# Four separate PSUM tiles for the block products of a fused attention and two-layer feed-forward kernel

## The chip, the cores and the metric

The kernel runs on one core of one Trainium2 chip. The metric is the device time of one execution in microseconds (us); less is better. The engines are TensorE (PE, matmuls; PEld is its weight loads), VectorE (DVE), ScalarE (ACT), GpSimd (POOL) and SyncE (SP, which only issues DMA transfers here).

## What is computed

Three steps in a row, all in float32 at the interface:

```
attn:  scores = q @ k^T / sqrt(D) + min(-(cum_i - cum_j), 0), causal, softmax, @ v
       B=2, H=8, S=576, D=64;  cum = cumsum(max(s, 0))
moe:   x = attn as (1152 tokens, 512);  xn = x / rms(x) * rms_g
       h = (silu(xn @ w_gate) * (xn @ w_val)) @ w_out          d_ff = 1536
moe2:  g = u * tanh(softplus(u)), u = h @ w_in;  out = g @ w_out   d_ff = 2048
```

The function `u * tanh(softplus(u))` is called Mish. The change lies in the third step.

## The kernel before

Matrices are held as pairs of numbers, a high and a low part (`xh` and `xl` for the activations, `w[:, 0]` and `w[:, 1]` for a weight unit), so that a product of two matrices takes three matmul passes: high by high, high by low, low by high (`PASS`, L567). The 1152 tokens are three blocks b = 0, 1, 2 of TB = 384 tokens.

The kernel first does the attention for eight pairs of heads, then the first feed-forward step, with the transfers and the unpacking of its weights beside it. All that is finished, and all weights are on the chip, before the part which the change touches.

In the third step the hidden dimension of 2048 is cut into NG = 8 sets (g = 0 to 7) of two chunks of 128. For each set and block three things are done:

- the inner product u (128 hidden rows x 384 tokens, two of them): `h2_mm` (L631), 24 matmuls of 384 columns, into a tile of two PSUM banks, and `mish` (L664) on ACT behind it;
- `mish_split` (L671): ACT casts the result to its high part, DVE subtracts to get the low part. Both go into one of two halves of the buffer `glb`; which half is chosen at L674;
- the out product, `out_mm` (L677): 18 matmuls of 512 columns, which accumulate over all eight sets into three row groups of 128 tokens (`o_t[b]`), each one bank. After set 7, `out_evac` (L694) copies the row groups to SBUF (ACT and DVE in turn) and SP issues the transfers to the output.

Block 0 does its inner products plainly for all eight sets. Blocks 1 and 2 do so only at set 0. For the sets 1 to 7 they are done together by `strassen` (L781), a scheme with seven products in place of eight for the 2 x 2 problem (two hidden chunks by two blocks, both cut in two along the contraction). `product` (L773) is six matmuls of 384 columns. The seven products go into four accumulators a, b, c and d; a, c and d take a second product on top of the first, with reads of the first in between:

1. product a (a11); ACT copies a into p (L792)
2. product b (s2); DVE adds p = p + b
3. product c (s3); DVE adds q = p + c
4. product d (s1); DVE adds q = q + d
5. a takes a12; ACT makes Mish of a (L806)
6. c takes a22, with t4 as its moving operand; DVE adds p + c, ACT makes Mish of it (L810)
7. d takes s4; DVE adds p = p + d, ACT makes Mish of p and q (L814)

The adds all stand on L717, in the helper `add`. The operands s1 to s4 of a set are sums of weight blocks (`s_restore`, `s_sums` on DVE, then `s_hi` on ACT, L767, and `s_lo` on DVE). They are made one set ahead: for the sets 2 to 6, `s_hi(g+1)` and `s_lo(g+1)` are issued in `gaps[0]`, that is behind product 1 of set g, and so ahead of the adds in DVE's queue. t1 to t4 are sums of activation blocks (`t_sums`, `t_split`); t4 lies in the first half of `glb`, and t3 takes the place of a part of block 2's activations, after the last plain product that reads them. In `gaps[3]` stands `mish_split(1, g-1)`. After each set's products comes `out_mm(1, g-1)`.

PSUM has eight banks. In this step they are three tiles of one bank in the pool `psT` (tag T), one of one bank in `psX` (tag X) and two of two banks each in `psS[1]` (tag S), which `banksS` (L558) hands out in turn. Before the change, a and b share one tile of S and c and d the other; the out product of block 0, and then that of block 1, has the three T tiles; that of block 2 has a pair of S and the X tile.

Each engine works off its instructions in the order in which the program issues them. Around the change this order is written out by hand (L988 to L1003 and the loop from L1014). A program adds the semaphores, which guard each tile against reading and overwriting too early.

Of the kernel before, what the change touches and what calls it, by code (L numbers as in the profile page):

```python
# [7 lines left out]
F32 = mybir.dt.float32  # L8
# [24 lines left out]
TB = 384  # L33
# [9 lines left out]
def tile_kernel(ctx: ExitStack, tc: tile.TileContext, kq, qq, v, s, w1, w2, rms_g, out):  # L43
    nc = tc.nc
    sb = ctx.enter_context(tc.tile_pool(name="sb", bufs=1))
    psT = ctx.enter_context(tc.tile_pool(name="psT", bufs=3, space=bass.MemoryType.PSUM))
    psX = ctx.enter_context(tc.tile_pool(name="psX", bufs=1, space=bass.MemoryType.PSUM))
# [6 lines left out]
    def sbt(shape, dt, tag, name):  # L54
        return sb.tile(shape, dt, tag=tag, name=name)
# [502 lines left out]
    def banksS():  # L558
        return psS[1].tile([128, 2, 512], F32, tag="S", name="gv")
# [66 lines left out]
    h2_t, u_t, g2_t, o_t = {}, {}, {}, {}  # L626

    def unit2(n):
        return unit(NU1 + n)

    def h2_mm(b, g):  # L631
        t = banksS()
        h2_t[b, g] = t
        for x in range(2):
            w = unit2(2 * (2 * g + x))
            n = 0
            for c in range(KD):
                for a, r in PASS:
                    nc.tensor.matmul(t[:, x, 0:TB], w[:, a, 128 * c:128 * c + 128],  # L639
                                     xhl[r][:, c, TB * b:TB * b + TB], start=(n == 0), stop=(n == 11))  # L640
                    n += 1

    NG = NF2 // 2
    glb = []
# [6 lines left out]
    def u_at(b, g):  # L651

        if (b, g) in u_t:
            return u_t[b, g]
        if b == 2 and g > 3:
            if not ub:
                ub.append(sbt([128, 4, 2, TB], F32, "w5", "ub"))
            u_t[b, g] = ub[0][:, g - 4]
        else:
            tag = ("mm", "ring8", "ring3", "ring5")[g] if b == 2 else ("hA", "hB")[g % 2] if b else                 ("hA", "hB", "mm")[g % 3]  # L660
            u_t[b, g] = sbt([128, 2, TB], F32, tag, "u")
        return u_t[b, g]

    def mish(b, g):  # L664
        nc.scalar.activation(out=u_at(b, g), in_=h2_t.pop((b, g))[:, :, 0:TB], func=ACTF.Mish)

    def split_pair(h, l, src):
        nc.scalar.copy(out=h, in_=src)  # L668
        nc.vector.tensor_tensor(out=l, in0=src, in1=h.bitcast(F32), op=ALU.subtract)  # L669

    def mish_split(b, g):  # L671
        if not glb:
            glb.append(sbt([128, 2, 2, 2, TB], F32R, "w6", "glb"))
        g2_t[b, g] = gl = glb[0][:, 1 if b == 1 else g % 2]  # L674
        split_pair(gl[:, 0], gl[:, 1], u_t.pop((b, g)))

    def out_mm(b, g):  # L677
        if g == 0:
            if b < 2:
                o_t[b] = [psT.tile([128, 512], F32, tag="T", name=f"o{n}") for n in range(3)]  # L680
            else:
                a0 = banksS()
                o_t[b] = [a0[:, 0], a0[:, 1], psX.tile([128, 512], F32, tag="X", name="o2")]
        gl = g2_t.pop((b, g))
        for tt in range(TB // 128):
            for x in range(2):
                w = unit2(2 * (2 * g + x) + 1)
                for y, (a, r) in enumerate(PASS):
                    nc.tensor.matmul(o_t[b][tt], gl[:, r, x, 128 * tt:128 * tt + 128], w[:, a],  # L689
                                     start=(g == 0 and x == 0 and y == 0), stop=(g == NG - 1 and x == 1 and y == 2))  # L690
# [3 lines left out]
    def out_evac(b):  # L694
        for tt in range(TB // 128):
            if b == 0 and tt < 2:
                if not ob:
                    ob.append(sbt([128, 2, 512], F32, "ring1", "osb"))
                t = ob[0][:, tt]
            else:  # L700
                t = sbt([128, 512], F32, f"r{(2 * b + tt + 2 * (b == 0)) % 4}", "osb")
            rows = slice(b * TB + 128 * tt, b * TB + 128 * tt + 128)

            cols = (slice(0, 256), slice(256, 512)) if (b, tt) == (NB - 1, 2) else (slice(0, 512),)
            for n, cs in enumerate(cols):
                if (tt + n) % 2 == 0:
                    nc.scalar.copy(out=t[:, cs], in_=o_t[b][tt][:, cs])
                else:
                    nc.vector.tensor_copy(out=t[:, cs], in_=o_t[b][tt][:, cs])
                nc.sync.dma_start(out=out[rows, cs], in_=t[:, cs])  # L710


    def quarter(r, c, b):
        return xhl[r][:, 2 * c:2 * c + 2, TB * b:TB * b + TB]

    def add(o, x, y, op=ALU.add):
        nc.vector.tensor_tensor(out=o, in0=x, in1=y, op=op)  # L717
# [28 lines left out]
    def t_split(n):  # L746
        tsum[n] = ((quarter(0, 0, 0), quarter(1, 0, 0)), (quarter(0, 1, 0), quarter(1, 1, 0)),
                   (quarter(0, 0, 2), quarter(1, 0, 2)), (glb[0][:, 0, 0], glb[0][:, 0, 1]))[n - 1]
        split_pair(*tsum[n], tq[n])

    def s_restore(g):

        c_t[g] = sbt([128, 1024], F32, "r1", "c")
        for x in range(2):
            w = unit2(4 * g + 2 * x).bitcast(F32)
            add(c_t[g][:, 512 * x:512 * x + 512], w[:, 0], w[:, 1])

    def s_sums(g):

        a11, a12, a21, a22 = (c_t[g][:, 256 * n:256 * n + 256] for n in range(4))  # L760
        for o, x, y, op in ((a22, a21, a22, ALU.add), (a21, a11, a21, ALU.subtract),
                            (a11, a22, a11, ALU.subtract), (a12, a12, a11, ALU.subtract)):
            add(o, x, y, op)

    def s_hi(g):
        s_t[g] = [sbt([128, 1024], F32R, t, f"s_{t}") for t in (("r0", "ring1"), ("r2", "r3"))[g % 2]]
        nc.scalar.copy(out=s_t[g][0], in_=c_t[g])  # L767

    def s_lo(g):
        h, l = s_t[g]  # L770
        add(l, c_t.pop(g), h.bitcast(F32), ALU.subtract)

    def product(t, A, B, start):  # L773
        n = 0
        for c in range(2):
            for a, r in PASS:
                nc.tensor.matmul(t, A[a][:, 128 * c:128 * c + 128], B[r][:, c], start=(start and n == 0),  # L777
                                 stop=(n == 5), skip_group_check=True)
                n += 1

    def strassen(g, gaps):  # L781

        w1_, w2_ = unit2(4 * g), unit2(4 * g + 2)
        s2, s4, s3, s1 = ([t[:, 256 * n:256 * n + 256] for t in s_t[g]] for n in range(4))
        a11, a12, a22 = ([w[:, a, o:o + 256] for a in range(2)] for w, o in ((w1_, 0), (w1_, 256), (w2_, 256)))
        x = {(c, b): (quarter(0, c, b), quarter(1, c, b)) for c, b in ((0, 1), (1, 1), (1, 2))}
        u1, u2 = u_at(1, g), u_at(2, g)
        p, q = u2[:, 0], u2[:, 1]
        t = banksS()
        a, b = t[:, 0, 0:TB], t[:, 1, 0:TB]  # L790
        product(a, a11, x[0, 1], True)
        nc.scalar.copy(out=p, in_=a)  # L792
        gaps[0]()
        product(b, s2, tsum[2], True)
        add(p, p, b)
        gaps[1]()
        t = banksS()
        c, d = t[:, 0, 0:TB], t[:, 1, 0:TB]
        product(c, s3, tsum[3], True)
        add(q, p, c)  # L800
        gaps[2]()
        product(d, s1, tsum[1], True)
        add(q, q, d)
        gaps[3]()
        product(a, a12, x[1, 1], False)
        nc.scalar.activation(out=u1[:, 0], in_=a, func=ACTF.Mish)  # L806
        gaps[4]()
        product(c, a22, tsum[4], False)
        add(u1[:, 1], p, c)
        nc.scalar.activation(out=u1[:, 1], in_=u1[:, 1], func=ACTF.Mish)  # L810
        gaps[5]()
        product(d, s4, x[1, 2], False)
        add(p, p, d)
        nc.scalar.activation(out=u2, in_=u2, func=ACTF.Mish)  # L814
# [73 lines left out]
    for p in range(NP):  # L888
# [9 lines left out]
        if NP - NA <= p:  # L898
            n = p - NP + NA
# [74 lines left out]
    for g in range(1, NG):  # L974
        h2_mm(0, g)
        mish_split(0, g - 1)
        mish(0, g)
        if g >= 2:
            out_mm(0, g - 2)
        w_tick()  # L980
        w_tick()
        if NG - 2 <= g:
            t_sums(g - NG + 2)
    for n in (2, 3, 4):
        t_sums(n)
    for n in (2, 1):
        t_split(n)
    out_mm(0, NG - 2)  # L988
    mish_split(0, NG - 1)
    t_split(4)  # L990
    s_restore(1)
    s_sums(1)
    h2_mm(1, 0)
    mish(1, 0)
    s_hi(1)
    s_lo(1)
    h2_mm(2, 0)
    mish(2, 0)
    t_split(3)
    s_restore(2)  # L1000
    s_sums(2)
    out_mm(0, NG - 1)
    out_evac(0)  # L1003

    def nothing():
        pass
# [75 lines left out]
```

## Time and profile before

| | us |
|---|---|
| three runs | 563.65, 564.43, 567.96 |
| their median | 564.43 |
| the profiled execution, its own time | 567.74 |
| its span, first to last instruction | 566.0 |
| PE busy in the span | 530.7 (94%) |
| DVE, ACT, POOL busy | 344.1, 268.0, 55.8 |

The profile is that of one execution. Matmuls are pipelined, and the profile shows a matmul as busy until its result is out, which is later than the start of the next one; so a busy PE isn't always a PE at its peak. The numbers of a row of the timeline are its start, its duration (for several merged instructions, from the first start to the last end), the engine, the line, the operation, the tiles (out<-in) and in brackets the idle time of the engine before it and what ended it. Names such as "gv" are those of tiles: every pair of banks from S is called gv, whatever it is used for.

### The profile page before, as it was taken

What the parts mean: (1) busy time and instruction counts of PE and PEld (TensorE: products, weight loads), DVE (VectorE), ACT (ScalarE), POOL (GpSimd) and SP (SyncE); (2) the same over time, 40 slices, a digit from 0 to 9 for tenths busy, and PEclk for the clock granted to TensorE, in tenths of its full rate; (3) what the DMA queues carried; (4) which work ended last, traced back from release to release, by engine and by line L of the source; (5) the groups of instructions that cost most, each with busy time, mean ns of one, the idle gap of its engine ahead of it and who ended that gap; (6) DMA issues with size and microseconds to landing.
All of it is one profiled execution on the core that took longest, in us unless ns stands there. A gap on an engine that the chain in (4) does not pass through costs nothing.

```text
span 566.0 us, 7923 instructions
## 1 busy us (share of the span) xinstructions
PE 530.7 (94%) x2966; PEld 474.8 (84%) x2966; DVE 344.1 (61%) x719; ACT 268.0 (47%) x596; POOL 55.8 (10%) x71
## 2 busy tenths in 40 slices
PE   5989998999999999999999999999998888888997
PEld 3767765688999999999999999989887777776785
DVE  7889999855545554555666475876785555532321
ACT  5767897866433433434454455554242222222221
POOL 5264545310000000000000000000000000000000
PEclk9989999999999999999999999999999999999999
DMA  9996985231423444434343053442001000000101
GB/s 231 258 257 164 260 205 122 76 115 54 129 76 113 140 121 118 142 113 142 98 133 112 2 148 112 117 138 81 0 20 38 1 0 1 0 1 0 57 0 56
DMA packets 18781, 55.90 MB, mean 99 GB/s; under 512 B 2348, under 2 KB 2604, under 8 KB 18716
## 3 DMA queue, kind: packets, MB, share of 16 engines
q1 hardware_dynamic: 13520, 42.04, 24.5%
q0 software_dynamic: 3712, 9.70, 8.4%
q10 hardware_dynamic: 1512, 3.66, 2.3%
q8 instruction: 23, 0.38, 0.3%
q14 instruction: 14, 0.11, 0.1%
HBM read 52.73 MB, written 2.66 MB: 98 GB/s over the span
## 4 chain that ended last, share of the span: by engine, by line
PE 80%; DVE 11%; ACT 5%; issue 3%; POOL 1%; DMA 0%; ACTq 0%; DVEq 0%; POOLq 0%
PE gv L584 25%; PE o L689 14%; PE y L615 8%; PE gv L777 8%; PE gv L639 7%; PE gv L615 4%; PE gv L689 4%; PE xa L473 3%; PE tp L435 2%; DVE sc L412 2%; PE sc L387 1%; PE sc L388 1%; DVE u L717 1%; ACT s_r L767 1%; ACT px L419 1%
## 5 line engine op out<-in xcount | busy, mean ns | idle before, releaser
L584 PE MATMUL gv<-xh,wring 128*128 128x384 f32 x576 | 147.6, 337 | 0.0
L584 PEld LDWEIGHTS gv<-xh,wring 128*128 128x128 f32 x576 | 104.0, 188 | 0.1
L584 PE MATMUL gv<-xl,wring 128*128 128x384 f32 x288 | 96.8, 336 | 0.0
L592 DVE TENSOR_TENSOR h_w<-h_w,gv 128x384 f32<-128x384 f32 x36 | 19.9, 553 | 62.5 <-ACT h_w L591 62.5
L591 ACT ACTIVATE h_w<-gv 128x384 f32<-128x384 f32 x36 | 17.7, 491 | 79.6 <-PE gv L584 79.6
L584 PEld LDWEIGHTS gv<-xl,wring 128*128 128x128 f32 x288 | 54.2, 188 | 0.0
L313 DVE SCALAR_TENSOR_TENSOR r<-r 128x512 int32<-128x512 int32 x68 | 51.3, 755 | 3.0
L615 PE MATMUL y<-hhl,w 128*128 128x384 f32 x288 | 50.5, 335 | 0.6 <-DVE hhl L598 0.6
L615 PEld LDWEIGHTS y<-hhl,w 128*128 128x128 f32 x288 | 49.9, 188 | 0.9 <-DVE hhl L598 0.9
L419 ACT ACTIVATE px<-sc,cst 128x384 f32<-128x384 f32 (+2 forms) x80 | 41.2, 524 | 10.3 <-DVE cst L412 10.0
L777 PE MATMUL gv<-xh,s_r 128*128 128x384 f32 x88 | 28.6, 362 | 14.7 <-DVE u L717 7.1
L306 ACT ACTIVATE r<-r 128x512 f32<-128x512 f32 x57 | 38.0, 671 | 3.6 <-DMA r<-in_w_dram 3.6
L435 PE MATMUL tp<-cst,px 128*128 128x128 f32 (+1 forms) x200 | 31.8, 288 | 4.8 <-DVE w L507 2.0
L412 DVE CUSTOM_DVE_ANT_0 sc<-sc,xtm 128x384 f32<-128x384 f32 (+4 forms) x72 | 34.5, 497 | 2.9 <-PE sc L388 2.1
L598 DVE TENSOR_TENSOR hhl<-h_w,hhl 128x384 fp32r<-128x384 f32 x36 | 19.8, 555 | 24.6 <-ACT hhl L597 24.6
L777 PEld LDWEIGHTS gv<-xh,s_r 128*128 128x128 f32 x88 | 16.2, 187 | 21.4 <-DVE u L717 10.3
L689 PE MATMUL o<-wt,glb 128*128 128x512 f32 x126 | 32.4, 392 | 1.5 <-ACT glb L668 1.0
L435 PEld LDWEIGHTS tp<-cst,px 128*128 128x128 f32 (+1 forms) x200 | 24.3, 146 | 10.9 <-issue 2.7
L597 ACT CAST hhl<-h_w 128x384 fp32r<-128x384 f32 x36 | 18.4, 516 | 31.7 <-PE y L615 18.2
L311 DVE TENSOR_SCALAR r<-r 128x512 int32<-128x512 int32 x68 | 32.8, 483 | 0.0
L689 PE MATMUL o<-w,glb 128*128 128x512 f32 x126 | 31.9, 391 | 0.0
L669 DVE TENSOR_TENSOR glb<-u,glb 128x768 fp32r<-128x768 f32 x20 | 19.0, 954 | 17.5 <-ACT glb L668 17.3
(185 smaller groups left out, 1017.6 us busy)
## 6 DMA issues: line engine op xcount, KB each, us to landing
r<-in_w_dram SPq DMA_DIRECT2D x66, 512.0 KB, 3.6
w<-in_kq_dram POOLq DMA_DIRECT2D x7, 576.0 KB, 6.3
w<-in_qq_dram POOLq DMA_DIRECT2D x7, 576.0 KB, 7.0
out_dram<-osb SPq DMA_DIRECT2D x8, 256.0 KB, 2.0
px<-in_v_dram SPq DMA_DIRECT2D x5, 320.0 KB
r<-in_w_dram ACTq DMA_DIRECT2D x2, 512.0 KB, 5.2
px<-in_v_dram ACTq DMA_DIRECT2D x3, 320.0 KB, 2.9
raw_hA<-in_kq_dram SPq DMA_DIRECT2D x3, 288.0 KB, 4.1
```

The lines of the kernel that those rows point to most:

```text
L306: nc.scalar.activation(out=top, in_=top, func=ACTF.Prelu, scale=2.0 ** -112, alpha=-2.0 ** 32)
L311: nc.vector.tensor_scalar(out=low, in0=low, scalar1=29, scalar2=None, op0=ALU.logical_shift_right)
L313: nc.vector.scalar_tensor_tensor(out=low, in0=top, scalar=3, in1=low, op0=ALU.logical_shift_left, op1=ALU.bitwise_or)
L412: nc.vector.tensor_tensor_reduce(out=sv, in0=sv, in1=m, scale=-0.125, scalar=first, op0=ALU.add, op1=ALU.min, accum_out=sbias[:, c:c + 1])
L419: nc.scalar.activation(out=pv, in_=sv, func=ACTF.Exp, bias=sbias[:, c + x:c + x + 1], scale=-1.0, accum_out=ssum[:, sc:sc + 1])
L435: nc.tensor.transpose(t[0:rows, o - a:o - a + 128], P[pos[i] % 2][:, o:min(e, o + 128)], ident)
L584: nc.tensor.matmul(t[:, g, 0:TB], w[:, a, 128 * c:128 * c + 128], xhl[r][:, c, TB * b:TB * b + TB], start=(n == 0), stop=(n == 11))
L592: nc.vector.tensor_tensor(out=h, in0=h, in1=t[:, 1, 0:TB], op=ALU.mult)
L615: nc.tensor.matmul(y_t[b][d], w[:, a, 128 * d:128 * d + 128], hhl[:, r], start=(f == 0 and y == 0), stop=(f == NF - 1 and y == 2))
L639: nc.tensor.matmul(t[:, x, 0:TB], w[:, a, 128 * c:128 * c + 128], xhl[r][:, c, TB * b:TB * b + TB], start=(n == 0), stop=(n == 11))
L689: nc.tensor.matmul(o_t[b][tt], gl[:, r, x, 128 * tt:128 * tt + 128], w[:, a], start=(g == 0 and x == 0 and y == 0), stop=(g == NG - 1 and ...
L777: nc.tensor.matmul(t, A[a][:, 128 * c:128 * c + 128], B[r][:, c], start=(start and n == 0), stop=(n == 5), skip_group_check=True)
```

## The change

Every block product gets a tile of its own: a, b and c one of the T tiles each, d the X tile. The out product of block 1 goes to the pairs of S in return, and that of block 2 to the three T tiles. The choice of `glb`'s half changes for blocks 1 and 2: block 1 keeps the second half but for its last set, which takes the first; block 2 begins with the second. In the plain products between set 0 and the first `strassen`, block 2 now comes first, then the last out product of block 0, then block 1 with the evacuation of block 0 behind it on the other engines.

```diff
@@ -671,16 +671,16 @@
     def mish_split(b, g):
         if not glb:
             glb.append(sbt([128, 2, 2, 2, TB], F32R, "w6", "glb"))
-        g2_t[b, g] = gl = glb[0][:, 1 if b == 1 else g % 2]
+        g2_t[b, g] = gl = glb[0][:, g % 2 if b == 0 else (g + 1) % 2 if b == 2 else g < NG - 1]
         split_pair(gl[:, 0], gl[:, 1], u_t.pop((b, g)))
 
     def out_mm(b, g):
         if g == 0:
-            if b < 2:
+            if b % 2:
+                a0, a1 = banksS(), banksS()
+                o_t[b] = [a0[:, 0], a0[:, 1], a1[:, 0]]
+            else:
                 o_t[b] = [psT.tile([128, 512], F32, tag="T", name=f"o{n}") for n in range(3)]
-            else:
-                a0 = banksS()
-                o_t[b] = [a0[:, 0], a0[:, 1], psX.tile([128, 512], F32, tag="X", name="o2")]
         gl = g2_t.pop((b, g))
         for tt in range(TB // 128):
             for x in range(2):
@@ -786,16 +786,14 @@
         x = {(c, b): (quarter(0, c, b), quarter(1, c, b)) for c, b in ((0, 1), (1, 1), (1, 2))}
         u1, u2 = u_at(1, g), u_at(2, g)
         p, q = u2[:, 0], u2[:, 1]
-        t = banksS()
-        a, b = t[:, 0, 0:TB], t[:, 1, 0:TB]
+        a, b, c = (psT.tile([128, 512], F32, tag="T", name=n)[:, 0:TB] for n in ("pa", "pb", "pc"))
+        d = psX.tile([128, 512], F32, tag="X", name="pd")[:, 0:TB]
         product(a, a11, x[0, 1], True)
         nc.scalar.copy(out=p, in_=a)
         gaps[0]()
         product(b, s2, tsum[2], True)
         add(p, p, b)
         gaps[1]()
-        t = banksS()
-        c, d = t[:, 0, 0:TB], t[:, 1, 0:TB]
         product(c, s3, tsum[3], True)
         add(q, p, c)
         gaps[2]()
@@ -990,17 +988,17 @@
     t_split(4)
     s_restore(1)
     s_sums(1)
-    h2_mm(1, 0)
-    mish(1, 0)
+    h2_mm(2, 0)
+    mish(2, 0)
     s_hi(1)
     s_lo(1)
-    h2_mm(2, 0)
-    mish(2, 0)
     t_split(3)
+    out_mm(0, NG - 1)
     s_restore(2)
+    h2_mm(1, 0)
+    out_evac(0)
+    mish(1, 0)
     s_sums(2)
-    out_mm(0, NG - 1)
-    out_evac(0)
 
     def nothing():
         pass
```

## Rows read from the trace of the kernel before

**Rows 1.** Windows, seven sets: stretch, us, PE, PEld, DVE, ACT, POOL busy, PEclk, DMA
```profile
436.26:450.79 14.53, 12.33 (x62) 10.56 (x60) 8.50 (x15) 4.03 (x6) 0.00 (x0) 1.00 0.00 1
...
508.62:522.78 14.16, 12.30 (x61) 10.38 (x59) 3.64 (x6) 3.08 (x5) 0.00 (x0) 1.00 0.00 0
sum 100.71, PE 86.02 PEld 73.75 DVE 49.04 ACT 27.81 POOL 0.00; mean PE 12.29 PEld 10.54 DVE 7.01 ACT 3.97 POOL 0.00
```

**Rows 2.** Groups by line, the seven sets: busy us, mean ns | idle before, releasers
```profile
L777 PE MATMUL gv<-xh,s_r 128*128 128x384 f32 x88 | 28.6, 362 | 14.7 <-DVE u L717 7.1 <-DVE ub L717 3.6 <-ACT ub L792 2.3
```

**Rows 3.** Tile gv, 422 to 530 us, who waited for it: us, times
```profile
  PE gv L777: 14.7, 21
```

**Rows 4.** Timeline of set 2
```profile
437.13 0.34 PE L777 MATMUL gv<-xh,wring 128*128 128x384 f32 x1
437.50 0.48 ACT L792 COPY u<-gv 128x384 f32<-128x384 f32 x1 [3.81 <-PE gv L777]
...
438.03 0.44 PE L777 MATMUL gv<-xh,s_r 128*128 128x384 f32 x1 [0.57 <-ACT u L792]
...
438.96 1.23 DVE L717 TENSOR_TENSOR s_r<-c,s_r 128x1024 fp32r<-128x1024 f32 x1 [1.85 <-ACT s_r L767]
...
440.10 1.21 DVE L717 TENSOR_TENSOR u<-u,gv 128x384 f32<-128x384 f32 x2
...
441.36 0.44 PE L777 MATMUL gv<-xh,s_r 128*128 128x384 f32 x1 [0.98 <-DVE u L717]
...
444.82 0.55 DVE L717 TENSOR_TENSOR u<-u,gv 128x384 f32<-128x384 f32 x1 [0.69 <-PE gv L777]
...
445.43 0.45 PE L777 MATMUL gv<-xh,s_r 128*128 128x384 f32 x1 [0.65 <-DVE u L717]
...
446.59 4.36 PE L689 MATMUL o<-wring,glb 128*128 128x512 f32 x18
```

**Rows 5.** Timeline, the last two out products of block 1
```profile
522.09 0.84 PE L689 MATMUL o<-wt,glb 128*128 128x512 f32 x3
523.02 1.57 ACT L668 CAST glb<-u 128x768 fp32r<-128x768 f32 x2 [2.74 <-PE o L689]
...
523.90 0.50 PE L689 MATMUL o<-wt,glb 128*128 128x512 f32 x1 [0.98 <-ACT glb L668]
...
524.89 4.15 PE L689 MATMUL o<-wt,glb 128*128 128x512 f32 x17 [0.49 <-DVE glb L669]
...
528.88 1.10 PE L689 MATMUL gv<-wring,glb 128*128 128x512 f32 x4
```

**Rows 6.** Timeline, the end of block 2's out product and its evacuation
```profile
560.46 1.52 PE L689 MATMUL o<-wt,glb 128*128 128x512 f32 x6
560.66 0.59 ACT L707 COPY osb<-gv 128x512 f32<-128x512 f32 x1 [5.96 <-PE gv L689]
...
562.02 0.37 ACT L707 COPY osb<-o 128x256 f32<-128x256 f32 x1 [0.77 <-PE o L689]
```

**Rows 7.** Timeline ahead of set 1 and at its start
```profile
417.95 4.28 PE L689 MATMUL o<-wt,glb 128*128 128x512 f32 x18
...
419.58 0.59 ACT L707 COPY osb<-o 128x512 f32<-128x512 f32 x1
...
421.92 1.80 DVE L717 TENSOR_TENSOR c<-c 128x256 f32<-128x256 f32 x4
...
423.64 0.68 DVE L709 COPY osb<-o 128x512 f32<-128x512 f32 x1
```

**Rows 8.** Windows, two stretches of earlier stages, columns as in rows 1
```profile
35.00:40.00 5.00, 5.00 (x28) 4.30 (x27) 4.36 (x18) 2.83 (x13) 2.16 (x3) 0.66 1.23 321
160.00:330.00 170.00, 169.41 (x978) 169.09 (x977) 95.62 (x178) 73.64 (x140) 0.00 (x0) 1.00 0.39 112
```

**Rows 9.** Timeline of PE, the same matmul in two stretches of attention
```profile
37.65 0.52 PE L388 MATMUL sc<-w 68*128 68x384 f32 x1
...
40.74 0.34 PE L388 MATMUL sc<-w 68*128 68x384 f32 x1
```

## Prediction

> **What bounds the kernel now.** I read the page first, with its chain of waits, then windows by stage, then the wait lists, then the timeline of single sets. The page puts PE on most of the chain, so the question for each stage is how much of it PE spends idle. The stage that the change touches is the seven sets (g = 1 to 7). They take 100.71 us, in which PE is busy for only 86.02 us [rows 1]; between 160 and 330 us it is busy for 169.41 of 170 us, with 978 matmuls, so a 384-column matmul is issued every 0.173 us there [rows 8]. The sets are therefore not at PE's rate, and what holds them is waits.
>
> The idle time sits ahead of the block products: 14.7 us, and its releasers are DVE's adds and ACT's copy, never a DMA [rows 2]. It comes in 21 pieces [rows 3], three for each of seven sets. The timeline of set 2, which begins at 436.26 [rows 1], shows which three [rows 4]:
> - Product b (s2) starts at 438.03, after 0.57 us idle, right behind ACT's copy of product **a** (437.50, 0.48 us). b doesn't read that copy. a and b share one tile of two banks, and that is all they share.
> - Product d (s1) starts at 441.36, after 0.98 us, right behind the second of the two adds that began at 440.10; that add reads **c**, d's tile mate.
> - Product d's second part (s4) starts at 445.43, after 0.65 us, right behind the add of 444.82, which again reads c.
> So the guard is by tile: an engine reading one half holds PE off the other half.
>
> **The change, part by part.**
>
> *1. Four tiles for a, b, c, d.* A stall costs more than the idle time shown. A matmul that ends a product lasts 0.34 us where the next would start 0.174 us after it (product a: six matmuls from 436.26, the last starting at 437.13, so 0.87/5 [rows 1, 4]): 0.16 us of drain lies under "busy". The first matmul after a stall lasts 0.44 instead of 0.34 [rows 4], as its weights come in behind the wait: 0.10 us more. The 21 stalls together: 14.7 + 21 x 0.26 = 20.2 us. Cross-check from starts: without stalls, set 2 is 42 matmuls x 0.174 = 7.3 us and then the 18 of the out product, 446.59 to 450.79 = 4.2 us [rows 1, 4], in all 11.5 instead of 14.53; seven sets 80.5 instead of 100.71 [rows 1]: 20.2 us again. That separate T tiles are guarded separately is seen at the first set: ACT evacuates o0 at 419.58 while PE is writing o1 and o2 (18 matmuls from 417.95, 4.28 us) [rows 7].
>
> What is late next? Waits that are real remain: the second part of a, c or d must follow the reading of its first part. Take set 2 with product a starting at 0 and a product taking 1.04 us.
> - The second part of a (a12) would start at 4 x 1.04 = 4.2; the copy ends at 437.98 - 436.26 = 1.7. Free.
> - The second part of c (a22) would start at 5 x 1.04 = 5.2. The add of c is held by DVE, not by PE: s_lo (438.96, 1.23 us) stands ahead of the adds in DVE's queue and waits for ACT's s_hi, which comes behind the copy, on the same clock as now. The adds run from 440.10 for 1.21 us, to 441.31 [rows 4], so to 5.05 after the set's start. PE follows 0.05 later (441.36), at 5.10. Margin 0.1 us, the narrowest of the set. A miss would cost the miss plus 0.26. Bounds per set 0 and 0.4 us in the five sets with an s_lo in that place (2 to 6), 0 to 2.0 in all; I take 0.4 in all, nearer to the row.
> - The second part of d (s4) would start at 6.2; the add of d, now third in DVE's queue, ends near 5.05 + 0.6 = 5.7. Free.
> - DVE is busy for 8.50 us of set 2 and less in the last one (3.64) [rows 1]; 8.50 still fits into 11.5.
> - The block 1 out product moves to the pairs of banks, which the sets no longer use. No engine reads them before the end, so it adds no wait.
>
> *2. The other half of glb for block 1's last split.* Now the split for (1, 7) goes into the half that out product (1, 6) is still reading. That out product's last three matmuls start from 522.09, so PE would be free at 522.09 + 3 x 0.23 = 522.78; ACT's cast starts only at 523.02, the next out product's first matmul follows at 523.90 and its other 17 at 524.89, until 528.88 [rows 5]. That is 6.10 us for work of 18 x (528.88 - 524.89)/17 = 4.2 us: 1.9 us lost. In the other half, which the products of t4 have left by then, the cast and the DVE split lie under the 4.2 us of out product (1, 6), and the split for (2, 0), in the first half's place, under that of (1, 7). I take -1.9; bounds -1.9 and -0.9 (the second wait alone stays, were the cast late).
>
> *3. Block 2's out product in three T tiles.* Its first row group is evacuated at 560.66 now, although PE has left it 6 matmuls (1.4 us) earlier, because it shares a pair [rows 6]. That will start sooner, but the end is set by the third row group, whose copy starts at 562.02 behind PE [rows 6]. Worth 0 to -0.4 (the last output transfers meet less traffic); I take -0.1.
>
> *4. The order of the plain groups.* The same matmuls are issued in the order h2(2, 0), out (0, 7), h2(1, 0) in place of h2(1, 0), h2(2, 0), out (0, 7). What it must cover is the freeing of the T tiles for a, b and c. Out (0, 7) now ends one h2 earlier, about 418.0, and h2(1, 0) covers 4.2 us behind it. The DVE copy of o1, which b needs, began at 423.64 behind the restores and sums [rows 7]; with s_sums(2) moved behind it (four adds, 1.80 us from 421.92 now [rows 7]) it would start at about 421.9 and, lasting 0.68 us, end near 422.6, and b starts at about 422.1 + 1.04 = 423.1. Hidden; if that cover failed it would cost about 1.2 us, once. ACT's mish(1, 0) also lands just ahead of set 1's copy. SP's three output issues of block 0 move with the copies, and s_hi(2), which reuses their buffers, is about 5 us later. I take +0.1, bounds 0 and +1.2.
>
> A rule that speaks against part 1: the chip shows a granted clock of 1.00 in all seven windows of the sets, although PE idles 21 times there [rows 1, 3]. The Trainium skill, page "TensorE: Matmul & The Clock Gate", section "A second HAM failure mode: psum-queue depth-cycling", says that cycling through PSUM banks can make PE idle briefly so often that its clock swings between two levels. No run here shows that for the sets. By the rule, four banks a set might lose what the waits give; by the rows, nothing. It is priced below as a rival.
>
> **Sum.** -20.2 + 0.4 - 1.9 - 0.1 + 0.1 = -21.7 us. The profiled execution took 567.74 us, with a span of 566.0; it would become 546.0, with a span of 544.3. It lies 3.3 us above the median of the three runs, 564.43; nothing ties that surplus to this stage, so I subtract from the median: **542.7 us**.
>
> **Rivals.**
> - *A new wait takes the place of the old.* The add of c comes late in sets 2 to 6 since s_lo, or the sums that feed it, slip by 0.5 us now that a set lasts 11.5 us and DVE needs 8.50: 5 x (0.5 + 0.26) = 3.8 us given back, 546.5. For it: the margin is 0.1 us. Against: s_hi and s_lo depend on the copy of a, which doesn't move.
> - *The guard is not what the tiles suggest.* PE's wait would be for the pool or for the order of instructions, so the 21 stalls stay; only parts 2 to 4 remain: 564.43 - 1.9 = 562.5. For it: the trace names releasers, not reasons. Against: o0 was evacuated beside PE's writing of o1 [rows 7].
> - *Slower: TensorE's clock.* Place: the seven sets. The level of 0.66 granted on average between 35 and 40 us [rows 8] holds stretches at 1.2 GHz; there a 68x384 matmul took 0.52 us, against 0.34 at 40.74 [rows 9]: 0.18 more. A set has 42 such matmuls and 18 of 512 columns (0.24 more each, in proportion): about 12 us more if all of it ran at the lower level, 83 us for seven. The gain of 21.7 is lost once 26% of the sets' matmuls run there; at half of them the time is 542.7 + 41 = 584. For it: only the rule above. Against: full clock through the busiest stretch (160 to 330) and through the idle-ridden sets alike [rows 1, 8].
>
> **How the numbers follow.** Forecast (all three waits gone, at most small remains) 0.74; a new wait 0.17; the guard unchanged 0.06; the clock 0.03. The first two are faster by over 1%, the bound that a measurement of this kernel can about tell from no change; the third is within it; the last is slower: 0.91, 0.06, 0.03. The range: the unknown terms reach from -22.5 (no remainder, best end) to -17.9 (remainders at their worst, cover of part 4 lost), and the runs of before spread from -0.8 to +3.5 about their median. That gives 541.1 to 550.0; I go half a microsecond lower for the rounding of the pitch. It holds the first two cases.
>
> **What would show it.** Right: each set takes 11.5 to 11.9 us, out products of block 1 are named gv, not o; PE's idle time ahead of the products falls from 14.7 us to under 2; out (1, 7) follows out (1, 6) without a gap; the DVE copy of o1 ends before set 1's product b. Wrong step by step: a wait on DVE's add ahead of a22 (margin gone), a wait of b on a DVE copy in set 1 (part 4), a cast between the last two out products of block 1 (part 2), a granted clock under 1.00 in the sets. The forecast as a whole is wrong if the sets stay above 13 us.

## The result and the profile after

The changed kernel took 545.75 us (median of four runs, 543.55 to 549.04) against 564.98 us for the kernel before in the same comparison (four runs, 563.65 to 567.96): a ratio of 0.966, 95% interval 0.959 to 0.972. It is faster, by 19.2 us, where 21.7 were forecast, and inside the range; the interval reaches from about 16 to 23 us and holds the forecast. By the time alone the first rival, a new wait in place of the old (546.5 us), lies nearer than the forecast of 542.7. What tells the two apart is the profile.

Run times of this kernel scatter by several microseconds, and the change is far smaller in some of the experiments below. So they are compared by a stretch of their profiles: from the first matmul of the plain product behind out product (0, 6) to the end of the span. Before it is 566.0 - 409.63 = 156.37 us, after it 545.0 - 410.23 = 134.77 us, 21.6 us less. What lies ahead of this stretch is the same program in all kernels, yet it ended between 404.6 and 410.2 us over twelve profiles. The three profiles in which it begins last (409.63 to 410.23: before, after and e3 below) are the three in which the granted clock fell between 30 and 50 us, to 0.91 on average; in the other nine it was 1.00 there, and the stretch begins between 404.62 and 409.07. So the difference between 21.6 and 19.2 has room ahead of the stretch; what else moves that start is not known. Inside the stretch the profiles repeat well: in the table below the column "plain" has two values only, apart from 0.01 us.

The windows of the seven sets after, in the columns of [rows 1]:

```profile
423.52:435.17 11.65, 11.65 (x61) 10.83 (x61) 8.21 (x15) 5.07 (x8) 0.00 (x0) 1.00 0.18 68
435.17:446.71 11.54, 11.54 (x62) 10.66 (x60) 8.90 (x17) 4.03 (x6) 0.00 (x0) 1.00 0.01 1
...
492.57:504.01 11.44, 11.44 (x62) 10.70 (x61) 4.60 (x7) 3.80 (x6) 0.00 (x0) 1.00 0.00 0
sum 80.49, PE 80.49 PEld 74.94 DVE 49.19 ACT 29.00 POOL 0.00; mean PE 11.50 PEld 10.71 DVE 7.03 ACT 4.14 POOL 0.00
```

80.49 us in place of 100.71, and PE is busy in all of it. The list of PE's waits from 422 us to the end, columns as "engine line, what it waited for: us in total, times, longest", has a single row, where [rows 3] counted 21 waits:

```profile
PE pa L777 <- ACT osb L707: 0.7, 1, 0.7
```

Set 2 in the timeline, to be laid beside [rows 4]:

```profile
436.22 0.34 PE L777 MATMUL pb<-xh,s_r 128*128 128x384 f32 x1
436.39 0.34 PE L777 MATMUL pb<-xl,s_r 128*128 128x384 f32 x1
436.42 0.48 ACT L792 COPY u<-pa 128x384 f32<-128x384 f32 x1 [3.51 <-PE pa L777]
...
437.88 1.23 DVE L717 TENSOR_TENSOR s_r<-c,s_r 128x1024 fp32r<-128x1024 f32 x1 [1.30 <-ACT s_r L767]
...
438.30 0.34 PE L777 MATMUL pd<-xh,s_r 128*128 128x384 f32 x1
...
439.67 0.55 DVE L717 TENSOR_TENSOR u<-u,pc 128x384 f32<-128x384 f32 x1
...
440.38 1.23 PE L777 MATMUL pc<-glb,wt 128*128 128x384 f32 x6
...
441.45 0.34 PE L777 MATMUL pd<-xh,s_r 128*128 128x384 f32 x1
```

Product b starts while ACT is still to read a, d starts 1.37 us ahead of the add that reads c, and none of these rows of PE has a bracket any more. The add of c ends at 440.22, 0.16 us before the second part of c begins: the forecast margin, 0.1 us, is there and just holds. The Trainium skill ("PSUM — Partial Sum Buffer", section "PSUM bank collisions raise a hardware error") asks for a guard by bank and quadrant, or by bank alone. This trace fits that: from 436.42 to 436.90 ACT reads a's bank while PE writes b's, and PE doesn't wait.

The end of block 1, beside [rows 5]: the cast no longer follows out product (1, 6), it lies in it, and PE runs from the one out product into the next (21 matmuls from 503.32 are three of the first and 18 of the second).

```profile
501.41 0.82 ACT L668 CAST glb<-u 128x768 fp32r<-128x768 f32 x1
...
503.32 4.92 PE L689 MATMUL gv<-wt,glb 128*128 128x512 f32 x21
...
508.08 7.18 PE L689 MATMUL o<-wring,glb 128*128 128x512 f32 x30
```

What had not been forecast stands at the start of set 1, beside [rows 7]:

```profile
422.51 0.34 PE L639 MATMUL gv<-xh,wring 128*128 128x384 f32 x1
422.88 1.07 ACT L707 COPY osb<-o 128x512 f32<-128x512 f32 x2 [3.49 <-PE gv L639]
422.88 0.69 DVE L709 COPY osb<-o 128x512 f32<-128x512 f32 x1 [0.90 <-PE gv L639]
...
423.52 0.44 PE L777 MATMUL pa<-xh,wring 128*128 128x384 f32 x1 [0.68 <-ACT osb L707]
```

The evacuation of block 0 doesn't run beside h2(1, 0), as the forecast had it. ACT sits idle for 3.49 us until that product is done, the copies then come at once (two on ACT, one on DVE), and product a waits for the first: 0.68 us.

### The profile page after: what moved, and what is told of

Read it like the earlier page. It is cut to its first block, busy times and chain, and to the rows that moved or that the text cites. A ratio compares the mean times of both kernels' runs of the same rounds, so it can differ in the third digit from the quotient of the medians.

```text
span 545.0 us, 7915 instructions
## 1 busy us (share of the span) xinstructions
PE 525.1 (96%) x2966; PEld 476.0 (87%) x2966; DVE 344.2 (63%) x719; ACT 267.3 (49%) x596; POOL 56.3 (10%) x71
## 4 chain that ended last, share of the span: by engine, by line
PE 84%; DVE 7%; ACT 3%; issue 3%; DMA 1%; POOL 1%; ACTq 0%; DVEq 0%; POOLq 0%
PE gv L584 26%; PE o L689 12%; PE y L615 8%; PE gv L639 8%; PE gv L689 6%; PE gv L615 4%; PE xa L473 3%; PE pa L777 3%; PE pc L777 3%; PE pd L777 3%; PE tp L435 2%; DVE sc L412 2%; PE pb L777 1%; DMA w<-in_qq_dram 1%; PE sc L387 1%
## 5 line engine op out<-in xcount | busy, mean ns | idle before, releaser
L473 PE MATMUL xa<-aw,px 128*64 128x320 f32 (+3 forms) x192 | 29.6, 377 | 0.0
L689 PE MATMUL o<-wt,glb 128*128 128x512 f32 x108 | 26.9, 390 | 0.0
L689 PE MATMUL o<-w,glb 128*128 128x512 f32 x108 | 26.5, 390 | 0.0
L615 PE MATMUL gv<-hhl,w 128*128 128x384 f32 x144 | 25.1, 334 | 0.0
```

Of the source, the lines that this page charges most:

```text
L473: nc.tensor.matmul(o, V[z][0:rows, c, ds], r, start=(c == 0), stop=(c == (1, 4)[part]))
L615: nc.tensor.matmul(y_t[b][d], w[:, a, 128 * d:128 * d + 128], hhl[:, r], start=(f == 0 and y == 0), stop=(f == NF - 1 and y == 2))
```

## The experiments

All twelve profiles by the same measure, one profile each; "plain" is from the start of the stretch to set 1, a set from its first matmul to that of the next. The last column is the one time or the median of the runs.

| kernel | stretch | plain | set 1 | set 3 | us |
|---|---|---|---|---|---|
| before | 156.37 | 12.44 | 14.19 | 14.46 | 564.98 |
| after | 134.77 | 13.29 | 11.65 | 11.43 | 545.75 |
| e1 order undone | 134.11 | 12.45 | 11.84 | 11.45 | 542.30 |
| e2 half of glb undone | 136.73 | 13.29 | 11.65 | 11.43 | 547.60 |
| e3 half of glb alone | 154.30 | 12.45 | 14.18 | 14.46 | 566.06 |
| e4 a and b in a pair | 140.18 | 12.45 | 13.00 | 12.25 | 548.27 |
| e5 c and d in a pair | 155.00 | 13.29 | 13.48 | 14.45 | 565.06 |
| e6 other output buffer | 133.87 | 12.45 | 11.54 | 11.44 | 541.25 |
| e7 old order, late sums | 133.68 | 12.45 | 11.52 | 11.41 | 541.41 |
| e8 split early | 138.03 | 13.29 | 11.65 | 12.08 | 548.59 |
| e9 e5 with late s_lo | 147.40 | 13.30 | 13.48 | 13.27 | 557.41 |
| e10 before with late s_lo | 154.48 | 12.45 | 14.17 | 14.15 | 561.95 |

**Is the guard by tile? One pair put back (e4).** a and b share a pair again, c and d keep tiles of their own; block 1's out product takes the other pair and the X tile. The tiles are taken once and kept for all sets.

```diff
-        a, b, c = (psT.tile([128, 512], F32, tag="T", name=n)[:, 0:TB] for n in ("pa", "pb", "pc"))
-        d = psX.tile([128, 512], F32, tag="X", name="pd")[:, 0:TB]
+        if not prod:
+            t = banksS()
+            prod.append([t[:, 0, 0:TB], t[:, 1, 0:TB]])
+            prod.append([psT.tile([128, 512], F32, tag="T", name=n)[:, 0:TB] for n in ("pc", "pd")])
+        (a, b), (c, d) = prod
```

> Stretch measured: from the first matmul of the plain product behind out (0, 6) to the end of the span; 156.4 us before the change, 134.8 after it. Guard by tile: with a and b in one pair and c and d apart, one wait a set returns, 0.57 us ahead of product b behind the copy of a, so 7 x (0.57 + 0.26) = 5.8 us more, stretch 140.6. Guard by pool or by order of the instructions: either no wait (134.8) or all of them (about 155).

The stretch came out at 140.18 us. PE's waits of this kernel:

```profile
PE gv L777 <- ACT u L797: 2.3, 3, 1.2
PE gv L777 <- ACT ub L797: 2.3, 4, 0.6
```

Seven waits, all for the copy of a, none for an add. The sets 2 to 7 have 0.57 us of idle each, and set 3 is 12.25 - 11.43 = 0.82 us longer: 0.25 on top of the idle, the drain and the weight load that the forecast had put at 0.26. Set 1 waits 1.21 us, since there the copy of a stands behind the copies of block 0 and a Mish in ACT's queue. The wait of product a ahead of set 1 is gone here (plain: 12.45), as a no longer has a T tile; so the 5.4 us of the stretch are 4.9 in the sets 2 to 7, 1.35 in set 1 and -0.84 ahead of it, and the closeness to the forecast 5.8 is in part chance. The guard is by tile: a and b wait for each other again where they share one, c and d don't where they have two. The releasers are read from semaphores, so it is the program's guard that shows here. What one wait costs is settled too. The timed ratio to the kernel before is 0.970 (0.967 to 0.974).

**Do the waits add up? The other pair put back (e5).** The mirror of e4: `prod` holds the pair for c and d and T tiles for a and b.

> c and d in one pair, a and b apart. Guard by tile, with the adds held by s_lo in sets 2 to 6: product b now comes 0.7 us earlier but the add of c ends 5.05 us after the set's start as before, so product d, ready at 3.13, starts at 5.10: 2.0 lost there plus 0.1, and 0.9 ahead of s4; in sets 1 and 7 0.9 and 0.9. Together 5 x 3.0 + 2 x 1.8 = 18.6 us, stretch 153.4. Rival, the 21 waits add up one by one: the 14 of c and d return 20.2 - 5.8 = 14.4 us, stretch 149.2.

155.00 us. In one place the clock disturbed it (below), for 16.01 - 14.48 = 1.5 us; without that it is 153.5, as the first theory had it and not as the sum of single waits. Set 3 takes 14.45 us, the same as before the change (14.46), although product b no longer waits. The rows are from set 2 (14.53 us in both kernels):

```profile
437.72 0.55 DVE L717 TENSOR_TENSOR u<-u,pb 128x384 f32<-128x384 f32 x1
438.37 0.56 DVE L717 TENSOR_TENSOR u<-u,gv 128x384 f32<-128x384 f32 x1
438.98 0.44 PE L777 MATMUL gv<-xh,s_r 128*128 128x384 f32 x1 [1.82 <-DVE u L717]
```

The wait ahead of d is now 1.82 us instead of 0.98: it has taken over the one ahead of b. The timed ratio to the kernel before is 0.999 (0.997 to 1.002); some of that is the clock's (last section). Half of the main edit, done on this side alone, would have been worth nothing in the sets that carry an s_lo.

**What holds the adds? (e9, e10)** In e9, the kernel of e5, and in e10, the kernel before, s_lo goes behind the add of c.

```diff
-            gaps[0] = doing((s_hi, g + 1), (s_lo, g + 1))
+            gaps[0] = doing((s_hi, g + 1))
+            gaps[2] = doing((s_lo, g + 1))
```

> c and d in one pair, a and b apart, s_lo behind the add of c in DVE's queue. If s_lo holds the adds, the wait ahead of d falls in sets 2 to 6 from 1.81 us to about 0.65, a set there from 14.5 to 13.3 us, five sets 6.0 us, stretch 153.5 - 6.0 = 147.5. Rival, the adds are late for another reason: sets stay at 14.5, stretch 153.5.

> The kernel before with s_lo behind the add of c. With a and b still paired, PE comes to d 0.8 us later, so s_lo costs only the 0.33 us by which the wait ahead of d is longer in sets 2 to 6 than in 1 and 7 (0.98 against 0.65): 5 x 0.33 = 1.7 us, sets 2 to 6 about 14.15, stretch 154.7. Rival, s_lo's place is worth as much here as with a and b apart (6 us): 150.4.

147.40 and 154.48 us, both within 0.3 of the forecast. In e9 the set is 13.27 us and every wait is at most 0.65:

```profile
PE gv L777 <- DVE u L717: 6.5, 10, 0.6
PE gv L777 <- DVE ub L717: 2.6, 4, 0.6
```

In e10 the two rows are the same, beside the seven waits for ACT's copy. The same move of one DVE instruction is worth 153.5 - 147.4 = 6.1 us where a and b are apart, and 156.37 - 154.48 = 1.9 us where they are not (5.8 and 1.6 of it in the sets 2 to 6). s_lo set when the add of c ended; the wait ahead of b hid most of that.

**How narrow is the margin ahead of a22? (e8)** The split of block 1, ACT's cast and DVE's subtraction, is issued earlier: `gaps[1] = doing((mish_split, 1, g - 1))` in place of `gaps[3]`. Its DVE half then stands ahead of the add of c.

> The split of block 1's last set (DVE 0.95 us) stands ahead of the add of c in DVE's queue. If that add has the narrow margin of 0.1 to 0.2 us ahead of a22, it ends about 0.85 later in sets 2 to 6, PE idles about 0.65 ahead of a22 and loses 0.26 more, 5 x 0.9 = 4.5 us, stretch 139.3; sets 1 and 7 lose nothing. If the margin is wide (over 1 us), nothing: 134.8.

```profile
438.02 0.95 DVE L669 TENSOR_TENSOR glb<-u,glb 128x768 fp32r<-128x768 f32 x1
...
438.89 0.55 DVE L717 TENSOR_TENSOR u<-u,pc 128x384 f32<-128x384 f32 x1
...
439.49 1.33 PE L777 MATMUL pc<-glb,wt 128*128 128x384 f32 x6 [0.41 <-DVE u L717]
```

PE's waits for that add, five in all:

```profile
PE pc L777 <- DVE ub L717: 1.2, 3, 0.4
PE pc L777 <- DVE u L717: 0.8, 2, 0.4
```

138.03 us: 3.3 more, in the five sets that have an s_lo and in no other. The expectation of 4.5 was too high in two places. The add ends only 0.68 us later relative to the set's start, not 0.85 (439.44 - 433.71 = 5.73 against 440.22 - 435.17 = 5.05), and the drain was counted twice, in the idle time and on top of it: the rows show 0.41 us idle, and a set grows by 0.65 (set 3: 12.08 - 11.43). But nearly all of the added delay shows: the margin is small, as forecast, and the changed kernel is at the edge there.

**The half of glb, both ways (e2, e3).** Only L674 is undone in the changed kernel, and only L674 is changed in the kernel before.

> The changed kernel with the old choice of glb's half. The wait behind out (1, 6) returns alone: 1.9 us, stretch 134.8 + 1.9 = 136.7, sets and plain products as in the changed kernel. Rival, the half is worth less now since ACT comes earlier: under 135.5.

> The kernel before with the new choice of glb's half alone. Out (1, 7) follows out (1, 6) without a gap: 1.9 us less, stretch 154.5, the sets as before (100.7). Rival, the cast is late for another reason than the half: 156.4.

136.73 - 134.77 = 1.96 us and 156.37 - 154.30 = 2.07 us. In e2 the two waits of [rows 5] are back:

```profile
PE gv L689 <- ACT glb L668: 1.0, 1, 1.0
...
PE gv L689 <- DVE glb L669: 0.5, 1, 0.5
```

e3 has neither. To 0.1 us, this part is independent of the others. In single times e3 was no faster than the kernel before (566.06 against 564.31): 2 us can't be told from its scatter by one run, but are plain in the stretch.

**The order of the plain products, undone (e1).** The third hunk of the change is taken back.

> New tiles and halves, the order of the plain products as before. The 0.68 us ahead of set 1's product a goes; product b then waits for the DVE copy of o1, which stands behind the restores and sums: about 1.2 us and 0.26. Stretch 134.8 - 0.9 + 1.4 = 135.3. Rival, the order carries part of the gain: over 137.

134.11 us, less than the changed kernel's 134.77. So the new order costs 0.66 us; it brings nothing. The expected wait was there, but small and at another product:

```profile
419.89 0.34 PE L777 MATMUL pb<-xh,s_r 128*128 128x384 f32 x1
...
420.40 0.68 DVE L709 COPY osb<-o 128x512 f32<-128x512 f32 x1
...
421.14 0.19 PEld L777 LDWEIGHTS pc<-xh,s_r 128*128 128x128 f32 x1 [0.37 <-DVE osb L709]
421.14 0.44 PE L777 MATMUL pc<-xh,s_r 128*128 128x384 f32 x1
```

Product b starts ahead of the DVE copy of o1; product c starts right behind its end at 421.08, and its weight load names that copy. So c, and not b, came by the bank of o1, the late copy met 1.04 us more cover, and set 1 is longer by only 11.84 - 11.52 = 0.32 us (against e7).

**Why the copies came late (e6).** The copies of o0 and o1 went into a buffer called ring1. The weight ring of that number holds a weight unit of set 0, which h2(1, 0) still reads in the new order. e6 gives o0 and o1 another buffer and leaves ring1 to o2:

```diff
-                    ob.append(sbt([128, 2, 512], F32, "ring1", "osb"))
+                    ob.append(sbt([128, 2, 512], F32, "r0", "osb"))
                 t = ob[0][:, tt]
+            elif b == 0:
+                t = sbt([128, 512], F32, "ring1", "osb")
```

> The copies of o0 and o1 go to two halves of the buffer r0, that of o2 to ring1. If they waited for h2(1, 0) since that product still reads its weights from ring1, ACT's copy of o0 starts over 2 us ahead of h2(1, 0)'s end, PE doesn't idle ahead of product a, stretch 133.9. Rival, they wait because they are issued behind h2(1, 0): the copy still starts at its end, 0.68 us idle, 134.8.

In this kernel the lines stand two further down.

```profile
416.26 0.59 ACT L709 COPY osb<-o 128x512 f32<-128x512 f32 x1 [1.48 <-DVE xl L669]
...
418.08 0.34 PE L779 MATMUL pa<-xh,wring 128*128 128x384 f32 x1
...
418.28 0.59 ACT L709 COPY osb<-o 128x512 f32<-128x512 f32 x1 [1.43 <-PE gv L639]
```

133.87 us. The first copy comes 1.8 us ahead of set 1 and 2.0 ahead of the end of h2(1, 0), product a doesn't wait, and the copy that still goes to ring1 is the one that waits for h2(1, 0). The place in the order is the same as in the changed kernel, so it was the buffer.

**The shortest stretch (e7).** The old order of the plain products, with s_sums(2) behind the evacuation of block 0, so that the DVE copy isn't held by it (the edit against e1):

```diff
     t_split(3)
     s_restore(2)
-    s_sums(2)
     out_mm(0, NG - 1)
     out_evac(0)
+    s_sums(2)
```

> Order of the plain products as before, but s_sums(2) behind the evacuation of block 0. ring1 is free by then, the DVE copy of o1 ends ahead of product b: no wait of PE in set 1, stretch 133.9, time about 0.9 us under the changed kernel's. Rival, a copy on ACT or the sums of set 2 become late: 134.8 or more.

133.68 us, and no wait of PE is left in the stretch. (e6 has none either, at 133.87; the 0.2 us between the two are too little to rank them.) The median of six runs is 541.41 us (539.63 to 543.61), the ratio to the kernel before 0.959 (0.955 to 0.963). It is 1.1 us better than the changed kernel by the stretch; the two ratios' intervals overlap, and the rest of the 4.3 us between the medians is not shown to be this edit's: in the profiled executions the stretch began at 405.5 against 410.2 us, after the same program.

## Why the prediction was right, step by step

- *Part 1, four tiles.* Right, and to the size: the sets were to take 80.5 us, they take 80.49, so 20.2 us as forecast. The guard by tile is shown by e4 and e5 from both sides, the 0.26 us on top of a stall by e4 (0.25). The 0.4 us set aside for the add of c was not needed; e8 shows that it was a near thing.
- *Part 2, the half of glb.* Right: 6.10 us became 508.08 - 504.01 = 4.07 (504.01 is 503.32 and three matmuls of 0.23), 2.0 against 1.9, and e2 and e3 give the same alone.
- *Part 3, block 2's tiles.* From the start of block 2's out product to the end of the span, 566.0 - 528.88 = 37.12 us became 545.0 - 508.08 = 36.92: 0.2 where 0.1 was taken. That gain is not shown. From the first matmul of that product to the end of its last it is 33.09 us in all twelve profiles, and from there to the end of the span 3.8 to 4.0 us in the three kernels with the old tiles (before, e3, e10) and 3.6 to 3.9 in the nine others. The first row group does leave earlier (its copy starts at 538.49 of 545.0, against 560.66 of 566.0), but the copy of the third still starts right behind PE, and the end hangs on it, as the forecast said. No run shows the reason it gave for a gain, less traffic at the end.
- *Part 4, the order.* Wrong. It was put at +0.1 as "hidden"; the plain products take 0.85 us more (against the old order in the new tiles, e1, it costs 0.66). The step that failed is that "h2(1, 0) covers 4.2 us behind" the last out product of block 0: this looked at who frees the T tiles, and not at where the copies write. Their target ring1 was still being read by the very product that was to be the cover (e6). The range's bound for this part, 1.2 us, held. The sign named for this fault, a wait of b on a DVE copy, was not the one that came: a waited for ACT's copy. The price given for the old order's fault was wrong as well: 1.2 us at product b in thought, 0.32 at product c in e1.
- *The sum.* -20.2 - 2.0 - 0.2 + 0.85 = -21.55, the 21.6 us of the stretch, against -21.7. The closeness is partly luck: the miss of part 4 and the reserve of 0.4 that wasn't used nearly cancel, and the 0.2 are within what the end of the span varies by.
- *The rivals.* A new wait in place of the old: none inside the sets, 0.16 us short of one, and s_lo didn't slip (the add of c ends 5.05 us after the start of set 2, as before); the one new wait stands ahead of them (part 4). The guard unchanged: excluded by the list of PE's waits. The clock: 1.00 in all seven windows, before the change with its 21 waits and after it with none of them; what the Trainium skill ("TensorE: Matmul & The Clock Gate", "A second HAM failure mode: psum-queue depth-cycling") describes was not seen in either. A fall of the clock did come in an experiment, below.

## What to carry to other kernels

Where two products shared a PSUM tile here, a reader of one held up the writer of the other, even in separate banks; count the pairs, not the banks. In this kernel each stall cost its idle time and about a quarter of a microsecond (e4, e8). Waits that follow one another in a loop need not add up: undoing one can lengthen the next to the same sum, so find what sets the last one (here an operation of another purpose in DVE's queue) before crediting a part of the edit. When a copy is moved to where a product is to hide it, ask of every operand, its target buffer too, who is still reading it.

## What the hardware showed that was not expected

In the profile of e5, the granted clock fell inside set 5, while the other sets, with the same waits, kept it at 1.00 (columns as in [rows 1]):

```profile
462.85:477.33 14.48, 12.02 (x62) 10.64 (x60) 7.68 (x13) 4.02 (x6) 0.00 (x0) 1.00 0.00 1
477.33:482.45 5.12, 3.31 (x19) 2.99 (x17) 2.24 (x3) 2.16 (x3) 0.00 (x0) 1.00 0.00 0
482.45:488.07 5.62, 4.97 (x19) 4.64 (x19) 1.98 (x3) 0.51 (x2) 0.00 (x0) 0.70 0.00 0
```

The rows of PE inside the last of these windows:

```profile
483.58 0.53 PE L777 MATMUL gv<-xh,s_r 128*128 128x384 f32 x1
483.90 0.53 PE L777 MATMUL pa<-xh,w 128*128 128x384 f32 x1
```

Ahead of the fall PE had been busy for 3.31 of 5.12 us and had waited for 1.81 us at a stretch. In it, 384-column matmuls start 0.32 us apart instead of 0.174, the lower level of 1.2 GHz, and the set lost 1.5 us. In this profile it happened in one set and not in the other four that have the same waits, and in none of the sets before the change, whose longest wait was 0.98 us. A loss of clock is not rare in this kernel: the mean granted clock of the profiled run, in which this is the only fall, is 0.997, and the ten timed runs of e5 have 0.991 to 0.997, while the four of e4 have 0.999 or 1.000 and the kernel before, timed beside them, 0.997 to 1.000. Most runs of e5 lost more than the profiled one; where in the run is not recorded. What the Trainium skill says at the place named above, that brief idling between groups of matmuls can make the clock swing, agrees with the fall in this one set, and four like it had none. Whether the length of the wait decides was not tried.
